# A three-layer kernel: in its last layer the second product takes blocks in another order, Sinkhorn steps are shared between two engines, and weight lows come two slots after highs

## The chip, the cores and the metric

One Trainium2 chip, of which one core runs the whole program. The metric is the time of one execution on the device in microseconds (us). The kernel before takes 1539.9 us, the median of three runs (1539.43 to 1543.54).

## The reference

Three layers follow one another. The first mixes a sequence in the frequency domain (FFT, complex product, shrinking, inverse FFT). The second sends each token to its best of 8 experts, with a capacity. The third, which the change touches, gives every token to every expert, weighted by a Sinkhorn-normalised matrix P:

```python
logits = x @ w_gate
logits = logits - logits.max()
P = np.exp(logits)
for _ in range(8):
    P /= P.sum(1, keepdims=True) + 1e-09
    P /= P.sum(0, keepdims=True) + 1e-09
    P *= N / E
out = np.zeros((N, D), dtype=np.float32)
for e in range(E):
    h = np.maximum(x @ w1[e], 0.0)
    ye = h @ w2[e]
    out += P[:, e:e + 1] * ye
```

Here N is 12288 tokens, of which 3072 slots (8 experts x 384) come out of the second layer with a value other than zero; D is 256, E 8, and 1024 hidden features per expert.

## The kernel before, in words

Products are made at single precision from halves: a value is split into a high part (rounded, in the type fp32r) and a low part (value minus high), and a product is high x high + high x low + low x high, three matmuls.

**Last layer.** The 3072 slots are held transposed, in two sides of 1536 columns. An expert is worked in two halves, and a half in three column tiles of 512, each with two parts `fp` of the features: six units per half, 98 units in all (the last half has its last tile cut into two of 256 columns, so it has eight). In this text units are numbered from 0; units 0 to 11 are the first expert, units 12 to 89 the thirteen halves after it, units 90 to 97 the last half. Within a half, the units of `fp` 0 are the even ones and those of `fp` 1 the odd ones.

The first product of a unit is a 2x2 block product done with seven products (Winograd's form of Strassen's scheme), one in each of seven slots (`PRODS`): three matmuls into a PSUM tile `ps_h` (three buffers). After each slot `post` (L1012) lets ScalarE, VectorE and GpSimd work on it: `plus` (L1032) adds the PSUM tile to a running sum `cc` on VectorE; `high` (L1020) makes the high part of a finished block with ReLU on ScalarE, for two of the four blocks with a second pass (L1022) that leaves ReLU in `cc`; `low` makes the low part, on GpSimd (L1027) or VectorE (L1029). The blocks have the names (f, side): (0,0), (1,1), (0,1), (1,0).

The second product (`second`, L961) of a unit runs in the seven slots of the next unit, three or four of its 24 matmuls behind the first product's three: each of the four blocks is multiplied with two column parts `c` of the weights into four PSUM banks `ps_y`, one per (c, side). The part `fp` 0 begins the banks and `fp` 1 ends them. So a bank begins in an odd unit. `seq` gives the order of the blocks. When a bank is complete, `evict` (L923) takes it out: VectorE multiplies with P (L932) into `yp`, and GpSimd adds that to `acc` (L933); for the first expert the bank is copied or added as it is, and `weigh0` (L937) multiplies it with P later, on GpSimd, in units 12 to 16. The four evictions of a pair of units lie in slots 5 and 6 of an even unit and slots 0 and 1 of the odd unit after it.

**Weights.** Two weight groups are made ready in each half: `load_r` loads one (SP's DMA queue), `sums_r` makes four sums of it on GpSimd (L750 to L753), `split_r` (L756) makes highs on ScalarE (L79) and lows on GpSimd (L80), in three parts.

**Sinkhorn.** After units 0 and 1 the logits' maximum is taken; from unit 2 on one step runs in slot 1 of each unit (`sink_a`, `sink_b`): row sums, a reciprocal, a multiplication of the 128 x 200 matrix `pr`, column sums over it, a matmul with ones that adds over partitions, a reciprocal and a second multiplication, all on VectorE but the matmul. `spread_p` writes P to DRAM, from where it is read back broadcast as `pb`.

**End.** For the last half `finish` (L941) transposes `acc` on TensorE, copies it on ScalarE and scatters rows to the output with indirect DMAs that GpSimd issues (L955), 24 of them.

What each engine does in what order is written out by hand: the code's order is each engine's order. A table of tasks, filled by `at(unit, slot, function)`, places what is not `post` behind a slot; evictions stand ahead of `post` in their slot, tasks behind it.

## Time and profile before

| what | us |
|---|---|
| median of 3 runs | 1539.9 (1539.43 to 1543.54) |
| the profiled execution, its own time | 1528.59 |
| its span, first to last instruction | 1526.7 |
| busy: TensorE matmuls, weight loads | 1433.6, 1198.7 |
| busy: VectorE, ScalarE, GpSimd | 1070.4, 697.4, 915.2 |

The profile is of one execution. Busy time is the sum of an engine's instructions. Its engines are PE (TensorE), PEld (its weight loads, which run beside the matmuls), DVE (VectorE), ACT (ScalarE), POOL (GpSimd) and SP (the queue of DMA issues). PEclk is the granted clock of TensorE as a share of its full speed. L27 would be line 27 of the kernel. A matmul's duration overlaps the next one's; start to start says what it costs.

### The profile page before, as it was taken

The page shows a single profiled execution, that of the slowest core. Times are in us where ns is not written, and L with a number is a line of the kernel's source. Part 1 is how long each engine was busy: PE and PEld are TensorE (multiplying, and loading weights), DVE is VectorE, ACT ScalarE, POOL GpSimd, SP SyncE. Part 2 cuts the span into 40 slices and gives each one's busy share as a digit, 9 for nine tenths or more (in the row PEclk, how much of TensorE's full clock was granted, in tenths as well). Part 3 has the DMA queues.
Part 4 walks back from the last instruction along what each step waited for, and adds up shares of the span by engine and source line. Part 5 has one row for each costly group of instructions (what it writes and reads, how often), then busy time and mean ns, then how long its engine had stood idle before and what let it go on. Part 6 is the DMA issues. An engine that isn't in the chain of part 4 may idle for free.

```text
span 1526.7 us, 20470 instructions
## 1 busy us (share of the span) xinstructions
PE 1433.6 (94%) x7102; PEld 1198.7 (79%) x7102; DVE 1070.4 (70%) x1790; ACT 697.4 (46%) x1326; POOL 915.2 (60%) x921
## 2 busy tenths in 40 slices
PE   8999897999999999999999999999999999999995
PEld 7988785999978777777877777787777778777774
DVE  4768787656579876767667676766767677676773
ACT  3444574555554444444444443444444444444441
POOL 2454356534553458766677677667766766776664
PEclk9999997999999999999999999999999999999997
DMA  9447752633201124322211111011101101110011
GB/s 243 118 127 187 199 173 66 191 104 111 84 28 29 42 72 132 130 72 80 83 44 45 37 42 42 29 42 50 46 31 42 42 31 39 56 42 15 28 53 45
DMA packets 82900, 117.10 MB, mean 77 GB/s; under 512 B 7078, under 2 KB 61190, under 8 KB 81350
## 3 DMA queue, kind: packets, MB, share of 16 engines
q1 hardware_dynamic: 67366, 93.74, 20.1%
q0 software_dynamic: 14656, 21.71, 5.5%
q8 instruction: 57, 0.93, 0.2%
q10 hardware_dynamic: 768, 0.28, 0.2%
q14 instruction: 53, 0.43, 0.1%
HBM read 87.29 MB, written 28.41 MB: 76 GB/s over the span
## 4 chain that ended last, share of the span: by engine, by line
PE 60%; POOL 12%; ACT 4%; DVE 4%; issue 3%; DMA 0%; POOLq 0%; DVEq 0%; ACTq 0%
PE ps_y L979 27%; PE ps_h L1089 24%; PE ps_h L686 4%; PE ps_yT L735 3%; POOL h L1027 3%; POOL acc L933 3%; POOL w L1027 2%; POOL w L80 2%; DVE cc L1032 2%; ACT cc L1022 1%; POOL zl L80 1%; ACT h L1020 1%; PE lg L700 1%; ACT w L79 1%; ACT w L1020 1%
## 5 line engine op out<-in xcount | busy, mean ns | idle before, releaser
L1032 DVE TENSOR_TENSOR cc<-ps_h,cc 128x512 f32<-128x512 f32 (+1 forms) x686 | 455.0, 677 | 288.4 <-PE ps_h L1089 273.7
L1020 ACT ACTIVATE h<-cc 128x512 fp32r<-128x512 f32 (+1 forms) x197 | 122.9, 624 | 338.0 <-DVE cc L1032 335.7
L933 POOL TENSOR_TENSOR acc<-acc,yp 128x512 f32<-128x512 f32 x162 | 236.5, 1473 | 21.7 <-DVE yp L932 21.7
L979 PE MATMUL ps_y<-h,w 128*128 128x512 f32 (+1 forms) x732 | 221.1, 392 | 8.2 <-POOL h L1027 8.2
L1089 PE MATMUL ps_h<-b_hi,w 128*128 128x512 f32 (+1 forms) x544 | 212.2, 391 | 0.0
L979 PEld LDWEIGHTS ps_y<-h,w 128*128 128x128 f32 x732 | 136.9, 193 | 42.1 <-POOL h L1027 13.7
L1089 PE MATMUL ps_h<-t_x,w 128*128 128x512 f32 (+1 forms) x544 | 168.2, 391 | 1.5 <-DVE cc L1032 1.5
L1020 ACT ACTIVATE w<-cc 128x512 fp32r<-128x512 f32 (+1 forms) x130 | 81.1, 624 | 192.0 <-DVE cc L1032 191.0
L1022 ACT ACTIVATE cc<-cc 128x512 f32<-128x512 f32 (+1 forms) x196 | 122.4, 625 | 6.2
L1089 PEld LDWEIGHTS ps_h<-t_x,w 128*128 128x128 f32 x544 | 102.2, 190 | 24.1 <-DVE cc L1032 1.9
L1089 PEld LDWEIGHTS ps_h<-b_hi,w 128*128 128x128 f32 x544 | 103.8, 191 | 21.9 <-DVE cc L1032 0.3
L932 DVE TENSOR_TENSOR yp<-ps_y,pb 128x512 f32<-128x512 f32 (+1 forms) x172 | 114.7, 667 | 7.0 <-PE ps_y L979 6.4
L979 PE MATMUL ps_y<-zl,w 128*128 128x512 f32 (+1 forms) x360 | 114.1, 389 | 5.0 <-POOL zl L1027 5.0
L979 PE MATMUL ps_y<-w 128*128 128x512 f32 (+1 forms) x274 | 104.4, 395 | 15.2 <-POOL w L1027 15.2
L979 PE MATMUL ps_y<-w,w 128*128 128x512 f32 (+1 forms) x266 | 101.7, 396 | 12.3 <-POOL w L1027 12.3
L80 POOL TENSOR_TENSOR w<-rw,w 128x128 fp32r<-128x128 f32 (+2 forms) x60 | 49.6, 840 | 95.7 <-ACT w L79 95.7
L1089 PE MATMUL ps_h<-b_lo,w 128*128 128x512 f32 (+1 forms) x272 | 106.2, 390 | 0.0
L979 PE MATMUL ps_y<-h,zl 128*128 128x512 f32 x320 | 97.8, 394 | 3.0 <-POOL h L1027 3.0
L1089 PE MATMUL ps_h<-b_hi,zl 128*128 128x512 f32 x240 | 95.1, 396 | 0.0
L979 PE MATMUL ps_y<-w,zl 128*128 128x512 f32 x240 | 80.8, 402 | 12.6 <-POOL w L1027 12.6
L1027 POOL TENSOR_TENSOR h<-cc,h 128x512 fp32r<-128x512 f32 (+1 forms) x66 | 86.7, 1323 | 5.5 <-ACT cc L1022 5.3
L979 PEld LDWEIGHTS ps_y<-zl,w 128*128 128x128 f32 x360 | 67.0, 191 | 22.2 <-POOL zl L1027 9.4
(265 smaller groups left out, 3271.3 us busy)
## 6 DMA issues: line engine op xcount, KB each, us to landing
pb<-p_d SPq DMA_DIRECT2D x44, 512.0 KB, 3.8
rw<-in_moe_w_dram SPq DMA_DIRECT2D x60, 256.0 KB, 3.1
raw<-in_moe_w_dram SPq DMA_DIRECT2D x26, 512.0 KB, 4.7
out_dram<-zt SPq DMA_DIRECT2D x24, 512.0 KB, 5.3
mf<-in_c_mats_dram POOLq DMA_DIRECT2D x40, 192.0 KB, 3.1
ds<-d SPq DMA_DIRECT2D x48, 128.0 KB, 2.8
xc<-ds SPq DMA_DIRECT2D x8, 768.0 KB, 6.2
xs_d<-xo SPq DMA_DIRECT2D x32, 192.0 KB, 3.1
```

The costliest lines, as they stand in the source:

```text
L79: nc.scalar.copy(hi_ap, src)
L80: (lo_engine or nc.vector).tensor_sub(lo_ap, src, hi_ap.bitcast(F32))
L686: nc.tensor.matmul(ps[:, 0:cap], l, r[:, h, :], start=k == 0, stop=k == 5)
L735: nc.tensor.matmul(yT[e][c], l, r, start=fk == 0 and i == 0, stop=fk == 2 * NF - 1 and i == 2)
L932: nc.vector.tensor_mul(y[:, 0:n], ps[:, 0:n], pbs[e, c0][:, side, 0:n])
L933: (nc.vector if last else nc.gpsimd).tensor_add(a, a, y[:, 0:n])
L979: yield lambda l=l, r=r, c=c, side=side, st=st, sp_=fp == 1 and k == final[side] and i == 2: nc.tensor.matmul(banks[c, side][:, 0:n], l, r ...
L1020: nc.scalar.activation(hs[f, side][0][:, 0:n], cc[k][:, 0:n], AF.Relu)
L1022: nc.scalar.activation(cc[k][:, 0:n], cc[k][:, 0:n], AF.Relu)
L1027: eng.tensor_sub(hl[:, 0:n], cc[k][:, 0:n], hh[:, 0:n].bitcast(F32))
L1032: nc.vector.tensor_add(cc[d][:, 0:n], ps[:, 0:n], cc[a][:, 0:n])
L1089: nc.tensor.matmul(ps[:, 0:n], l, x_[:, c0:c0 + n], start=k == 0, stop=k == 2)
```

## The change

- The second product takes the blocks as (0,0), (1,1), (1,0), (0,1), for both parts `fp`. Products six and seven of the first product change places, and with them the slots in which (1,0) and (0,1) are finished. Evictions take side 0 ahead of side 1.
- GpSimd's low of block (1,1) moves from slot 5 to slot 4. VectorE's lows are now (1,0) in slot 6 and (0,1) in slot 0 of the next unit.
- In the last half all lows and all additions to `acc` are VectorE's, and ScalarE's second pass is left out there.
- A Sinkhorn step stands in three places of a unit (slots 1, 3 and 6), and GpSimd does its two multiplications.
- Evictions of the first expert's second half are a copy on ScalarE and an addition on GpSimd, in place of an addition on VectorE.
- `split_r` issues the highs of a part in one slot and its lows two slots later; the sums move from slot 0 to slot 3.
- The transposes of `finish` use the PSUM tile of the small products for all but one in two, and stand in every second slot.

Instructions by engine, counted in the two programs. VectorE has 16 multiplications of `pr` and 12 additions from PSUM fewer; it has 8 block lows of 512 and 8 of 256 columns more, and 6 additions to `acc` more (4 of 512 columns, 2 of 256). GpSimd gives up those lows and those 6 additions and gets the 16 multiplications and 12 additions to `acc`. ScalarE has 12 copies of a bank more and 16 second passes fewer. TensorE's matmuls are the same in number, and the DMA issues of SP and GpSimd the same in number and order.

The diff, cut to its core:

```diff
-    def split_r(r, t, u, part):
+    def split_r(r, t, u, part, which=None):
...
-            split(w[:, o:o + n], w[:, WN + o:WN + o + n], src, nc.gpsimd)
+            if which != 1:
+                nc.scalar.copy(w[:, o:o + n], src)
+            if which != 0:
+                nc.gpsimd.tensor_sub(w[:, WN + o:WN + o + n], src, w[:, o:o + n].bitcast(F32))
...
-    def sink_a():
+    def sink_a1():
...
-        nc.vector.tensor_tensor(pr, pr, rs.unsqueeze(2).to_broadcast([128, NT + 1, E]), op=ALU.mult)
+        nc.gpsimd.tensor_tensor(pr, pr, rs.unsqueeze(2).to_broadcast([128, NT + 1, E]), op=ALU.mult)
+
+    def sink_a2():
         cs = hp.tile([128, E], F32, tag="cs", name="cs", bufs=2)
...
-    def sink_b(cs):
+    def sink_b():
...
-        nc.vector.tensor_tensor(pr, pr, rc.unsqueeze(1).to_broadcast([128, NT + 1, E]), op=ALU.mult)
+        nc.gpsimd.tensor_tensor(pr, pr, rc.unsqueeze(1).to_broadcast([128, NT + 1, E]), op=ALU.mult)
...
+        y = hp.tile([128, BL], F32, tag="py", name="yp", bufs=3)
         if e == 0:
-            nc.vector.tensor_add(a, ps[:, 0:n], a)
+            nc.scalar.copy(y[:, 0:n], ps[:, 0:n])
+            nc.gpsimd.tensor_add(a, a, y[:, 0:n])
             return
...
-        seq = [((1, 1), (0, 1), (0, 0), (1, 0)), ((0, 0), (1, 1), (0, 1), (1, 0))][fp]
+        seq = ((0, 0), (1, 1), (1, 0), (0, 1))
...
-    PRODS = ((0, B11), (4, T2), (1, B21), (5, T3), (3, T1), (6, B22), (2, T4))
+    PRODS = ((0, B11), (4, T2), (1, B21), (5, T3), (3, T1), (2, T4), (6, B22))
...
-                at(first + 1, 0, lambda r=r: sums_r(r))
-                for k, i in enumerate((0, 4, NS + 2)):
-                    at(first + 2, i, lambda r=r, k=k: split_r(r, rws[r], sus[r], k))
+                at(first + 1, 3, lambda r=r: sums_r(r))
+                for k, i in enumerate((1, 3, NS + 1)):
+                    for which in range(2):
+                        at(first + 2, i + 2 * which, lambda r=r, k=k, which=which: split_r(r, rws[r], sus[r], k, which))
...
-    for k, fn in enumerate(sink):
-        at(2 + k, 1, fn)
-    n_s = 2 + len(sink)
+    at(2, 1, sink_exp)
+    for k in range(ITERS):
+        at(2 + k, 3, sink_a1)
+        at(2 + k, 6, sink_a2)
+        at(3 + k, 1, sink_b)
+    at(2 + ITERS, 4, spread_p)
+    n_s = 4 + ITERS
...
+        end = units[u][0:2] == (E - 1, 1)
+        mid = nc.vector if end else nc.gpsimd
...
-            low(0, 0, 0, nc.gpsimd)
+            low(0, 0, 0, mid)
         elif i == 4:
             plus(3, 2)
-            high(3, 1, 1)
+            high(3, 1, 1, not end)
             plus(1, 1)
+            low(3, 1, 1, mid)
         elif i == 5:
+            plus(2, 2)
+            high(2, 1, 0)
+        else:
             plus(1, 1)
             high(1, 0, 1)
-            low(3, 1, 1, nc.gpsimd)
-        else:
-            plus(2, 2)
-            high(2, 1, 0)
-            low(1, 0, 1, nc.vector)
-            at(u + 1, 0, lambda: low(2, 1, 0, nc.vector))
+            low(2, 1, 0)
+            at(u + 1, 0, lambda: low(1, 0, 1))
...
-                when = {(0, 1): (u, 5), (1, 1): (u, 6), (0, 0): (u + 1, 0), (1, 0): (u + 1, 1)}
+                when = {(0, 0): (u, 5), (1, 0): (u, 6), (0, 1): (u + 1, 0), (1, 1): (u + 1, 1)}
```

How the order of instructions moves, at three places. In the names, `cc` are running sums, `h0` to `h4` and the upper ends of `w1`, `w2` and `zl` the six buffer pairs of highs and lows, `rw` and `su` weights as loaded and their sums, `ps_y_...` PSUM banks.

GpSimd in unit 44, the third of a half, and the first part of unit 45, before. The block lows are lines L1027, those of (0,0) and (1,1) in turn:

```order
L80 TENSOR_TENSOR w2_7237<-rw_12787,w2_7237 128x128
L80 TENSOR_TENSOR w2_7237<-rw_12787,w2_7237 128x256
L1027 TENSOR_TENSOR w1_7236<-cc_12961,h4_8958 128x512
L80 TENSOR_TENSOR w2_7237<-su_12876,w2_7237 128x512
L933 TENSOR_TENSOR acc_8953<-acc_8953,yp_13021 128x512
L1027 TENSOR_TENSOR w2_7237<-cc_13006,w1_7236 128x512
L933 TENSOR_TENSOR acc_8953<-acc_8953,yp_13034 128x512
L933 TENSOR_TENSOR acc_8953<-acc_8953,yp_13048 128x512
L933 TENSOR_TENSOR acc_8953<-acc_8953,yp_13066 128x512
L80 TENSOR_TENSOR w2_7237<-rw_12787,w2_7237 128x512
```

And in the changed kernel, where block lows are L1031, weight lows L764, additions L931:

```order
L1031 TENSOR_TENSOR w1_7236<-cc_12985,h4_8958 128x512
L764 TENSOR_TENSOR w2_7237<-rw_12811,w2_7237 128x128
L764 TENSOR_TENSOR w2_7237<-rw_12811,w2_7237 128x256
L1031 TENSOR_TENSOR w2_7237<-cc_13031,w1_7236 128x512
L931 TENSOR_TENSOR acc_8953<-acc_8953,yp_13045 128x512
L764 TENSOR_TENSOR w2_7237<-su_12940,w2_7237 128x512
L931 TENSOR_TENSOR acc_8953<-acc_8953,yp_13058 128x512
L931 TENSOR_TENSOR acc_8953<-acc_8953,yp_13072 128x512
L931 TENSOR_TENSOR acc_8953<-acc_8953,yp_13091 128x512
L1031 TENSOR_TENSOR h1_8955<-cc_13075,h0_8954 128x512
L764 TENSOR_TENSOR w2_7237<-rw_12811,w2_7237 128x512
```

The low of (1,1), `w2_7237<-cc_...`, stood behind the weight low of `su` and an addition; now it stands ahead of both, and behind the two small weight lows.

TensorE at the start of unit 45, before, the first matmuls of the second product (of unit 44); `w2_7237` as the moving operand's name is the low of (1,1):

```order
L979 MATMUL ps_y_13044<-w1_7236,zl_2920 128x512
L979 MATMUL ps_y_13044<-w2_7237,zl_2920 128x512
L979 MATMUL ps_y_13044<-w1_7236,zl_2920 128x512
L1089 MATMUL ps_h_13057<-t_x_7330,w1_7236 128x512 x3
L979 MATMUL ps_y_13061<-w1_7236,zl_2920 128x512
L979 MATMUL ps_y_13061<-w2_7237,zl_2920 128x512
L979 MATMUL ps_y_13061<-w1_7236,zl_2920 128x512
L979 MATMUL ps_y_13044<-w2_7237,zl_2920 128x512
L1089 MATMUL ps_h_13071<-b_hi_7328,w1_7236 128x512
L1089 MATMUL ps_h_13071<-b_lo_7329,w1_7236 128x512
L1089 MATMUL ps_h_13071<-b_hi_7328,w1_7236 128x512
L979 MATMUL ps_y_13044<-zl_2920 128x512
```

And in the changed kernel, where `h4` and `w1` are high and low of (0,0), and `w1` and `w2` those of (1,1):

```order
L978 MATMUL ps_y_13068<-h4_8958,zl_2920 128x512
L978 MATMUL ps_y_13068<-w1_7236,zl_2920 128x512
L978 MATMUL ps_y_13068<-h4_8958,zl_2920 128x512
L1095 MATMUL ps_h_13081<-t_x_7330,w1_7236 128x512 x3
L978 MATMUL ps_y_13085<-h4_8958,zl_2920 128x512
L978 MATMUL ps_y_13085<-w1_7236,zl_2920 128x512
L978 MATMUL ps_y_13085<-h4_8958,zl_2920 128x512
L978 MATMUL ps_y_13089<-w1_7236,zl_2920 128x512
L1095 MATMUL ps_h_13097<-b_hi_7328,w1_7236 128x512
L1095 MATMUL ps_h_13097<-b_lo_7329,w1_7236 128x512
L1095 MATMUL ps_h_13097<-b_hi_7328,w1_7236 128x512
L978 MATMUL ps_y_13089<-w2_7237,zl_2920 128x512
```

The block (0,0) is now first, the low of (1,1) is read for the first time behind 16 other matmuls of the unit, and the seventh matmul of the second product begins a bank of the other side; the bank after it begins at the tenth.

VectorE at the end of unit 92 and the start of unit 93, in the last half, before (multiplications L932, lows L1029, additions to `acc` L933):

```order
L932 TENSOR_TENSOR yp_17247<-ps_y_17104,pb_17138 128x512
L1032 TENSOR_TENSOR cc_17204<-ps_h_17239,cc_17204 128x512
L932 TENSOR_TENSOR yp_17260<-ps_y_17118,pb_17138 128x512
L1032 TENSOR_TENSOR cc_17224<-ps_h_17253,cc_17224 128x512
L1029 SCALAR_TENSOR_TENSOR zl_2920<-cc_17204,w2_7237 128x512
L932 TENSOR_TENSOR yp_17274<-ps_y_17146,pb_17138 128x512
L933 TENSOR_TENSOR acc_8953<-acc_8953,yp_17274 128x512
L1029 SCALAR_TENSOR_TENSOR zl_2920<-cc_17224,zl_2920 128x512
L932 TENSOR_TENSOR yp_17289<-ps_y_17157,pb_17138 128x512
L933 TENSOR_TENSOR acc_8953<-acc_8953,yp_17289 128x512
```

And in the changed kernel (L927, L1033, L929):

```order
L927 TENSOR_TENSOR yp_17266<-ps_y_17126,pb_17161 128x512
L929 TENSOR_TENSOR acc_8953<-acc_8953,yp_17266 128x512
L1036 TENSOR_TENSOR cc_17243<-ps_h_17258,cc_17243 128x512
L927 TENSOR_TENSOR yp_17278<-ps_y_17140,pb_17161 128x512
L929 TENSOR_TENSOR acc_8953<-acc_8953,yp_17278 128x512
L1036 TENSOR_TENSOR cc_17224<-ps_h_17271,cc_17224 128x512
L1033 SCALAR_TENSOR_TENSOR zl_2920<-cc_17243,w2_7237 128x512
L927 TENSOR_TENSOR yp_17292<-ps_y_17144,pb_17161 128x512
L929 TENSOR_TENSOR acc_8953<-acc_8953,yp_17292 128x512
L1033 SCALAR_TENSOR_TENSOR zl_2920<-cc_17224,zl_2920 128x512
L927 TENSOR_TENSOR yp_17308<-ps_y_17157,pb_17161 128x512
L929 TENSOR_TENSOR acc_8953<-acc_8953,yp_17308 128x512
```

Each of the four multiplications of an eviction now has its addition behind it on VectorE; one low stands ahead of the third multiplication and one between the third and the fourth, as before.

## Rows read from the trace of the kernel before

**Rows 1.** windows by stage of the last layer: span, then busy us (instructions), PEclk, DMA, GB/s
```profile
422.65:555.36 132.71, 125.78 (x557) 100.16 (x556) 109.01 (x205) 64.90 (x119) 61.68 (x61) 1.00 0.12 38
555.36:1422.16 866.80, 826.51 (x3512) 662.43 (x3511) 616.42 (x859) 376.03 (x650) 597.51 (x529) 0.99 0.17 54
1443.39:1526.70 83.31, 61.24 (x343) 54.04 (x341) 44.77 (x83) 26.43 (x55) 42.85 (x42) 0.85 0.13 45
```

**Rows 2.** windows of units 42 to 47, then of unit 51
```profile
889.30:899.59 10.29, 10.29 (x47) 8.45 (x46) 8.11 (x12) 4.86 (x8) 5.95 (x6) 1.00 0.11 32
899.59:910.51 10.92, 10.67 (x47) 8.37 (x46) 8.57 (x12) 4.28 (x7) 10.20 (x11) 1.00 0.21 68
910.51:920.80 10.29, 10.29 (x46) 8.44 (x45) 7.06 (x12) 5.35 (x10) 3.35 (x4) 1.00 0.00 0
920.80:935.75 14.95, 12.24 (x47) 9.51 (x46) 7.79 (x12) 4.87 (x8) 11.37 (x10) 0.89 0.18 64
935.75:946.15 10.40, 10.40 (x46) 8.44 (x45) 7.25 (x12) 4.34 (x7) 5.35 (x7) 1.00 0.03 11
946.15:956.80 10.65, 10.65 (x47) 8.36 (x45) 8.34 (x12) 5.25 (x10) 8.96 (x8) 1.00 0.14 49
...
988.30:1001.58 13.28, 10.57 (x47) 8.37 (x45) 7.76 (x12) 4.87 (x8) 11.30 (x10) 1.00 0.20 70
```

**Rows 3.** waits of TensorE in units 12 to 89: total us, times, longest
```profile
PE ps_y L979 <- POOL w L1027: 35.3, 13, 2.7
PE ps_y L979 <- POOL h L1027: 5.0, 13, 1.9
```

**Rows 4.** timeline of GpSimd at unit 45: start us, us, line, operation
```profile
919.90 1.30 POOL L80 TENSOR_TENSOR w<-su,w 128x512 fp32r<-128x512 f32 x1 [2.18 <-ACT w L79]
921.17 1.72 POOL L933 TENSOR_TENSOR acc<-acc,yp 128x512 f32<-128x512 f32 x1
922.85 1.71 POOL L1027 TENSOR_TENSOR w<-cc,w 128x512 fp32r<-128x512 f32 x1
```

**Rows 5.** timeline of TensorE at unit 45
```profile
924.61 0.73 PE L979 MATMUL ps_y<-w,zl 128*128 128x512 f32 x2 [2.71 <-POOL w L1027]
```

**Rows 6.** timeline of ScalarE in unit 43
```profile
905.80 0.63 ACT L1022 ACTIVATE cc<-cc 128x512 f32<-128x512 f32 x1
```

**Rows 7.** timeline of VectorE at the start of unit 43
```profile
899.76 1.65 DVE L1029 SCALAR_TENSOR_TENSOR w<-cc,h 128x512 fp32r<-128x512 f32 x1
901.33 0.68 DVE L932 TENSOR_TENSOR yp<-ps_y,pb 128x512 f32<-128x512 f32 x1
901.93 1.18 DVE L1029 SCALAR_TENSOR_TENSOR w<-cc,w 128x512 fp32r<-128x512 f32 x1
903.03 0.68 DVE L932 TENSOR_TENSOR yp<-ps_y,pb 128x512 f32<-128x512 f32 x1
```

**Rows 8.** timeline of VectorE, its longest and its shortest low
```profile
603.56 1.78 DVE L1029 SCALAR_TENSOR_TENSOR w<-cc,w 128x512 fp32r<-128x512 f32 x1
...
910.62 0.68 DVE L1029 SCALAR_TENSOR_TENSOR h<-cc,h 128x512 fp32r<-128x512 f32 x1
```

**Rows 9.** waits of TensorE in units 0 to 11
```profile
PE ps_y L979 <- POOL w L1027: 3.1, 2, 1.7
PE ps_y L979 <- POOL h L1027: 2.0, 1, 2.0
```

**Rows 10.** groups by line, units 0 to 11: busy us, mean ns, idle before
```profile
L845 DVE TENSOR_TENSOR pr<-pr,rs 128x200 f32<-128x200 f32 x8 | 2.9, 367 | 0.3
...
L80 POOL TENSOR_TENSOR w<-rw,w 128x256 fp32r<-128x256 f32 x2 | 1.5, 744 | 0.0
```

**Rows 11.** group of VectorE from 1443.39 on, and timeline of the last matmuls
```profile
L1032 DVE TENSOR_TENSOR cc<-ps_h,cc 128x256 f32<-128x256 f32 x28 | 11.4, 422 | 14.5 <-PE ps_h L1089 14.3
...
1510.76 2.45 PE L979 MATMUL ps_y<-h,w 128*128 128x256 f32 x12
```

More of the change, by code (lines that the diff above doesn't have):

```diff
@@ L848, in sink_a @@
         nc.vector.scalar_tensor_tensor(cs, pr[:, NT, :], WZ, cs, op0=ALU.mult, op1=ALU.add)
-        return cs
-    def sink_b(cs):
+        state["cs"] = cs
+    def sink_b():
         ps = pq.tile([128, NT, 2 * E], F32, tag="s", name="ps_s")
-        nc.tensor.matmul(ps[:, 0, 0:E], ones_f, cs, start=True, stop=True)
+        nc.tensor.matmul(ps[:, 0, 0:E], ones_f, state["cs"], start=True, stop=True)
         rc = hp.tile([128, E], F32, tag="rc", name="rc", bufs=2)
@@ L857, in sink_b @@
         nc.vector.tensor_scalar_mul(rc, rc, float(N // E))
-        nc.vector.tensor_tensor(pr, pr, rc.unsqueeze(1).to_broadcast([128, NT + 1, E]), op=ALU.mult)
+        nc.gpsimd.tensor_tensor(pr, pr, rc.unsqueeze(1).to_broadcast([128, NT + 1, E]), op=ALU.mult)
     state = {}
-    def sink_rows():
-        state["cs"] = sink_a()
-    def sink_cols(last):
-        sink_b(state["cs"])
-        if not last:
-            sink_rows()
-    sink = [lambda: (sink_exp(), sink_rows())] + [lambda k=k: sink_cols(k == ITERS - 1) for k in range(ITERS)]
     p_d = dr.tile([E, S], F32, name="p_d")
@@ L927, in evict @@
             return
+        y = hp.tile([128, BL], F32, tag="py", name="yp", bufs=3)
         if e == 0:
[L929 removed]
+            nc.scalar.copy(y[:, 0:n], ps[:, 0:n])
+            nc.gpsimd.tensor_add(a, a, y[:, 0:n])
             return
[L931 removed]
         nc.vector.tensor_mul(y[:, 0:n], ps[:, 0:n], pbs[e, c0][:, side, 0:n])
[L933 removed]
+        if last:
+            nc.vector.tensor_add(a, a, y[:, 0:n])
+        else:
+            nc.gpsimd.tensor_add(a, a, y[:, 0:n])
     def weigh0(c, side, c0):
@@ L941, in finish @@
     def finish(c0, side, g):
-        pt = ph.tile([128, 2, D], F32, tag="h", name="ps_o")
+        pt = (pq.tile([128, 2, D], F32, tag="s", name="ps_o") if len(outs) != 1 else
+              ph.tile([128, 2, D], F32, tag="h", name="ps_o"))
         if not outs:
@@ L1014, in tile_c, with high @@
             return hp.tile([128, BL], F32, tag="cc", name="cc", bufs=5)
-        def high(k, f, side):
+        def high(k, f, side, also=False):
             nonlocal npair
@@ L1020, in high, with low @@
             nc.scalar.activation(hs[f, side][0][:, 0:n], cc[k][:, 0:n], AF.Relu)
-            if k in (0, 3):
+            if also:
                 nc.scalar.activation(cc[k][:, 0:n], cc[k][:, 0:n], AF.Relu)
-        def low(k, f, side, eng):
+        def low(k, f, side, eng=nc.vector):
             hh, hl = hs[f, side]
@@ L1069, in tile_spectral_mix__moe_topk__moe_sinkhorn @@
             last = (pe_, ph_) == (E - 1, 1)
-            fins = [(side, g) for side in (1, 0) for g in range(pn // 256)]
+            fins = [(side, g) for side in (0, 1) for g in range(pn // 256)]
             if u == NU2:
-                when = {(c, side): (u, NS) for c in range(2) for side in range(2)}
+                when = {(c, side): (u, NS) for side in range(2) for c in range(2)}
             else:
-                when = {(0, 1): (u, 5), (1, 1): (u, 6), (0, 0): (u + 1, 0), (1, 0): (u + 1, 1)}
+                when = {(0, 0): (u, 5), (1, 0): (u, 6), (0, 1): (u + 1, 0), (1, 1): (u + 1, 1)}
             for (c, side), (uu, i) in when.items():
                 soon.setdefault((uu, i), []).append(
-                    lambda c=c, side=side, a=(pe_, ph_, pc, pn), last=last and (side == 0 or u == NU2): evict(*a, c, side, banks[c, side], last))
+                    lambda c=c, side=side, a=(pe_, ph_, pc, pn), last=last: evict(*a, c, side, banks[c, side], last))
             if last:
                 for k, (side, g) in enumerate(fins):
-                    at(u + 1, (3 if u < NU2 else 0) + k, lambda pc=pc, side=side, g=g: finish(pc, side, g))
+                    at(u + 1, 3 + 2 * k if u < NU2 else k, lambda pc=pc, side=side, g=g: finish(pc, side, g))
         if u < NU2 and fp == 0 and e > 0:
```

8 lines of the change are left out of this document (3 added, 5 removed).

## The prediction

> **What bounds the kernel now.** I read the windows by stage first. The last layer runs from 422.65 to 1526.70 us of the span, 72% of it, and in its long middle, units 12 to 89, TensorE is busy for 826.5 of 866.8 us [rows 1]. TensorE sets the end there; the question is what its lost time is. The six units of one half of an expert answer it: they do equal work (45 matmuls of 512 columns) and take 10.29, 10.92, 10.29, 14.95, 10.40 and 10.65 us; the fourth of the next half takes 13.28 [rows 2]. I take 10.28 us as the undisturbed unit (0.2285 us a matmul). The long ones are the second, fourth and sixth (the odd units), and the longest has a granted clock of 0.89, where the next half's fourth has 1.00. The 78 units of the middle then hold 78 x 10.28 = 801.8 us of matmuls, and 65.0 us are lost, 5.0 per half.
>
> The waits of TensorE name who ends it: 40 us on GpSimd's lows [rows 3], in each half 2.7 us in the fourth unit and about 0.4 in the second. The timeline shows why. GpSimd runs a weight low (L80), an accumulation (L933) and only then the block low (L1027), which ends at 924.56 [rows 4]; TensorE does one matmul of the second product, waits 2.71 us and starts again at 924.61 [rows 5], for a stretch at the lower of its two levels, 1.2 GHz, by the granted clock of that unit [rows 2]. The low is that of block (1,1), made late and by the even units consumed first. The second unit's wait leaves the clock at 1.00, and so does the long wait of the next half: 14.95 against 13.28 us says that a fall costs 1.6 us where it comes.
>
> **The change, part by part.** *Order of the blocks and of GpSimd's queue.* In the third unit of a half the low of (1,1) moves from behind a weight low of 1.30 and an addition of 1.72 us to ahead of both, and its first reader moves from number 1 to number 7 (counted from 0) of the next unit's second product, with 16 matmuls or 3.7 us of that unit ahead of it; the block read at once is now (0,0), whose low stands first. The low of (0,0) can start when ScalarE's second pass ends, 906.43 in the unit that began at 899.59, so 6.8 us into a unit [rows 6]; at 1.3 us it ends at 8.1 and is needed at 10.5. Two small weight lows, at most 1.5 us together by the larger one's 0.74 [rows 10], follow, then low (1,1), until 10.9 at the latest, needed at 13.9. Both are early by 2 us or more. Four 128x128 sums in their place, at most 3.0 us by the same row, leave 1.5. So the waits of rows 3 should go. The queue still holds the same work: 46 of 66.7 us a half [rows 1]; what is late next is an addition, for which only PSUM banks wait.
>
> *Those banks are the new wait.* Each odd unit starts the next use of four banks. The pair evicted last was needed at matmuls 12 and 15 of the second product; now it is needed at matmuls 6 and 9, that is 12 and 18 matmuls into the unit: 2.74 and 4.11 us. VectorE's queue there is low, multiplication, low, multiplication, unchanged. In the unit that starts at 899.59 the two multiplications end at 902.01 and 903.71, or +2.42 and +4.12 us [rows 7]. So the second one is just in time. A low takes 0.68 us alone and up to 1.78 [rows 8]; the unit of rows 7 had 1.65 + 1.18. From below the cost is nothing; from above, with 1.78 twice, the end moves by 0.73 to +4.85, a wait of 0.74 in 39 odd units, 29 us. I take 0.5 us per half, 6.5 us, near the lower end, the side that the rows of such a place lie on [rows 7].
>
> The rule that speaks against the change is in the Trainium skill, "SBUF — State Buffer", section "Who interferes with whom": a VectorE instruction with two SBUF inputs and a GpSimd instruction that reads SBUF exclude each other, and the later one blocks until the other ends. The trace agrees in kind (0.68 against 1.78 us). By the row the term is 6.5 us; by the rule, with a whole GpSimd instruction ahead of every low, it would be the 44 us of rival 2.
>
> Units 12 to 17 also carry the 12 weighing multiplications on GpSimd; I leave them 2 us of waits. Middle: 65.0 - 6.5 - 2 = **56.5 us** gained.
>
> *Weight lows two slots after the highs, sums later.* No operation is added. GpSimd no longer stands waiting for a copy that ScalarE has not begun; that idle time ended nothing by itself, so I count it at nothing beyond the above. The target buffer is free throughout: its last reader is done a unit earlier. SP's and GpSimd's DMA issues keep their order and number, so no transfer moves past another.
>
> *Sinkhorn and first expert (units 0 to 11).* They take 132.7 us against 123.4, 9.3 more; TensorE's waits for GpSimd's lows are 5.1 of them [rows 9], the rest is extra TensorE work there (logits, sums over partitions) and a first wait. VectorE loses two multiplications of 0.37 us per step [rows 10] and twelve additions from PSUM. GpSimd gets them, ScalarE a copy ahead of each addition; ScalarE is busy for 64.9 of these 132.7 us [rows 1] and takes it beside other work. What a 128x200 multiplication costs on GpSimd no row shows: between VectorE's 0.37 and the 0.74 of a 128x256 subtraction on GpSimd [rows 10], I take 0.7, nearest to the row of its own engine. New waits: TensorE's product for the column sums now comes two slots after those sums, which VectorE makes behind a low. With rows 7 the low ends at +1.74, the reduction and its correction (two instructions of 0.37 or little more) at +2.6 at the latest, and TensorE arrives at +2.97. That is no wait; if GpSimd delivers its multiplication 1 us late in each of eight steps it is 8 us. Between -2 and +7 I take **5 us** gained, nearer the upper end, because the multiplication has three slots, some 4.4 us, for its 0.7.
>
> *Last half and tail.* From 1443.39 to the end there are 83.3 us [rows 1] at a granted clock of 0.85. The change puts all lows and all additions on VectorE. From there its queue holds 38 instructions of 512 columns at 0.69 and 52 of 256 at 0.42 [rows 7, 11]: 26.2 + 21.8 = 48.0 us. TensorE's own matmuls up to the last product, at 0.2285 us and half of it for 256 columns, are 20.6 + 7.9 + 15.4 = 43.9 us, so VectorE becomes the bound there. With 2.3 us until its first instruction (nine matmuls), 4 for waits on ScalarE's highs, 2 for the last product and the 13.5 us from its last matmul (1513.2 [rows 11]) to the end, I get 69.8, 13.5 less. I take **12 us**, since waits around 2 us appear where both engines are full and may cost a stretch at 1.2 GHz. Bounds: 2 if the clock falls as often as now, 17 if nothing waits.
>
> **Sum.** 56.5 + 5 + 12 = 73.5 us. The profiled execution took 1528.6 us (span 1526.7), so it should become 1455. The median of the runs shown is 1539.9, 0.7% above it; I keep the difference: 1466.
>
> **Rivals.**
> 1. *Banks wait at the rows' maximum.* 29 us in the middle instead of 6.5, Sinkhorn 3, tail 9: 34 + 12 = 46 gained, 1494. For it: the second multiplication has no slack in rows 7. Against: a low alone takes 0.68 [rows 8].
> 2. *Every VectorE low waits for a whole GpSimd instruction*, 0.68 + 1.29 = 1.97. To the 2.83 us of the two lows of rows 7 that adds 1.11 us per odd unit, 43 to 44 in all: 19 + 12 = 31 gained, 1509. For it: lows of 1.65 and 1.78 exist [rows 7, 8]. Against it: none reaches 1.97. [...]
> 3. *The bank wait grows over 2.1 us and lowers the clock.* With both lows behind a GpSimd instruction that was itself held (1.72), they take 2.4 each and the second multiplication ends at +6.1. 39 x 2.0 is 78 us against 65 + 17 gained at best; from 2.1 us per odd unit on it is a loss. If every second wait costs 1.6 us of clock as now, 31 more: 27 slower, 1567. For it: three such waits a half instead of one. Against: the longest low of the rows is 1.78 [rows 8].
> 4. *The change doesn't do what it says:* the lows are held by ScalarE's second pass rather than by GpSimd's queue, and TensorE waits as before; 1536 to 1541. Against: GpSimd worked from 919.90 to 924.56 without a gap [rows 4].
>
> **How the numbers follow.** Forecast 0.70, rival 1 0.15, rival 2 0.07, rival 3 0.04, rival 4 0.03, more than the best bounds 0.01. The forecast's best case is 65 + 8 + 17 = 90 us, 1450; its poor case 54, 1486. The range takes in rival 1 and the worst of the bounds: 1449 to 1500. About 0.3% (4.6 us) can be told from no change: faster 0.93, same 0.03, slower 0.04.
>
> **What would show it.** Right: the odd units at 10.3 to 10.6 us, no wait of TensorE on GpSimd's lows in the middle, granted clock 1.00 there, units 12 to 89 near 810 us. Rival 1 or 2: waits of the second product's matmuls on VectorE's multiplication, 0.5 to 1.1 us in odd units, lows over 1.7. Wrong on Sinkhorn: TensorE waiting for the column sums. Wrong on the tail: more than 72 us from unit 92 on. A middle above 840 us refutes the forecast.

## Result and profile after

The changed kernel takes 1472.9 us, the median of four executions (1469.51 to 1474.01), beside 1540.1 for the kernel before: a ratio of 0.9556, interval 0.9534 to 0.9577. The forecast was 1466 with a range from 1449 to 1500. The profiled execution took 1472.11 us.

The windows of the changed kernel by stage of the last layer (units 0 to 11, 12 to 89, 90 and 91, 92 to the end); the columns are those of [rows 1]:

```profile
435.99:562.95 126.96, 124.49 (x556) 100.55 (x556) 101.22 (x181) 68.64 (x127) 78.75 (x86) 1.00 0.16 51
562.95:1375.99 813.04, 810.97 (x3511) 656.66 (x3510) 622.89 (x855) 380.53 (x654) 586.68 (x532) 1.00 0.17 56
1375.99:1397.18 21.19, 20.93 (x91) 16.82 (x90) 18.28 (x27) 6.63 (x11) 8.37 (x7) 1.00 0.07 26
1397.18:1469.90 72.72, 57.46 (x343) 49.52 (x341) 48.65 (x101) 20.77 (x43) 24.54 (x24) 0.93 0.15 51
```

Against [rows 1] the middle gives 53.8 us, the first expert 5.75, the end 10.6; the whole last layer goes from 1104.05 to 1033.91 us, 70.1 less. TensorE is now busy for 811.0 of the middle's 813.0 us. One number does not belong to the change: the last layer starts at 435.99, where it started at 422.65. The code ahead of it is the same; the last section comes back to it.

The windows of units 42 to 47, which answer to [rows 2], and of unit 14:

```profile
878.26:888.54 10.28, 10.28 (x47) 8.45 (x45) 7.89 (x12) 4.89 (x8) 5.21 (x6) 1.00 0.04 12
888.54:899.02 10.48, 10.48 (x46) 8.37 (x45) 8.44 (x12) 4.29 (x7) 9.40 (x10) 1.00 0.28 90
899.02:909.32 10.30, 10.30 (x46) 8.44 (x45) 7.50 (x12) 5.36 (x10) 4.59 (x6) 1.00 0.00 1
909.32:919.62 10.30, 10.30 (x47) 8.37 (x45) 8.36 (x12) 4.88 (x8) 10.30 (x8) 1.00 0.16 52
919.62:930.02 10.40, 10.40 (x46) 8.44 (x45) 7.26 (x12) 4.34 (x7) 4.86 (x8) 1.00 0.15 50
930.02:940.46 10.44, 10.44 (x47) 8.37 (x45) 8.41 (x12) 5.36 (x10) 9.44 (x8) 1.00 0.15 50
583.64:597.76 14.12, 12.19 (x46) 9.51 (x45) 7.50 (x12) 5.41 (x10) 13.08 (x15) 0.88 0.53 151
```

The fourth unit, 14.95 us before, takes 10.30, at a granted clock of 1.00. The reason is in GpSimd's timeline around the end of unit 44, which answers to [rows 4]:

```profile
907.92 1.30 POOL L1031 TENSOR_TENSOR w<-cc,w 128x512 fp32r<-128x512 f32 x1 [0.55 <-ACT cc L1026]
909.17 1.30 POOL L931 TENSOR_TENSOR acc<-acc,yp 128x512 f32<-128x512 f32 x1
910.43 1.75 POOL L764 TENSOR_TENSOR w<-su,w 128x512 fp32r<-128x512 f32 x1
```

The low of (1,1) ends at 909.22, 10.20 us into its unit (899.02), where it ended 14.05 us into it before; it waits for ScalarE alone, and the addition and the weight low stand behind it. Three lines of the waits in the middle are what is left for the second product (one more, of 0.6 us, stands at a weight load); [rows 3] had 40.3 us on GpSimd's lows at the matmuls:

```profile
PEld ps_y L978 <- DVE yp L927: 9.2, 38, 0.3
PEld ps_y L978 <- POOL zl L1031: 2.3, 1, 2.3
PE ps_y L978 <- POOL zl L1031: 1.9, 1, 1.9
```

The first line is the forecast's new wait, for the banks, in 38 odd units, 0.24 us each; it is so short that it shows at the weight loads and not at the matmuls. The other two are one wait on a low of GpSimd, in unit 14, the last of the windows above; the part on why the prediction was right comes back to it. VectorE's timeline at the start of unit 43 (888.54), which answers to [rows 7]:

```profile
888.71 1.62 DVE L1033 SCALAR_TENSOR_TENSOR w<-cc,h 128x512 fp32r<-128x512 f32 x1
890.25 0.68 DVE L927 TENSOR_TENSOR yp<-ps_y,pb 128x512 f32<-128x512 f32 x1
890.85 1.18 DVE L1033 SCALAR_TENSOR_TENSOR w<-cc,w 128x512 fp32r<-128x512 f32 x1
891.95 0.68 DVE L927 TENSOR_TENSOR yp<-ps_y,pb 128x512 f32<-128x512 f32 x1
```

The two multiplications end 2.39 and 4.09 us into the unit and are needed at 2.74 and 4.11, to a few hundredths what [rows 7] had.

Of the signs that the prediction named, the odd units (10.29 to 10.49 us) and the middle (813) came as it said. Two did not: TensorE does wait once for a low of GpSimd, in unit 14, where the clock falls to 0.88, and the end, at 72.7 us, lies just beyond the 72 that it called wrong.

### The profile page after: what moved, and what is told of

Read it like the earlier page. It is cut to its first block, busy times and chain, and to the rows that moved or that the text cites. A ratio compares the mean times of both kernels' runs of the same rounds, so it can differ in the third digit from the quotient of the medians.

```text
span 1469.9 us, 20547 instructions
## 1 busy us (share of the span) xinstructions
PE 1415.6 (96%) x7102; PEld 1188.3 (81%) x7102; DVE 1074.7 (73%) x1784; ACT 697.1 (47%) x1322; POOL 896.0 (61%) x927
## 4 chain that ended last, share of the span: by engine, by line
PE 70%; issue 5%; POOL 5%; DVE 1%; ACT 1%; DMA 0%; POOLq 0%; DVEq 0%; ACTq 0%
PE ps_y L978 32%; PE ps_h L1095 28%; PE ps_h L686 5%; PE ps_yT L735 4%; POOL out_dram L954 1%; PE lg L700 1%; POOL acc L925 1%; POOL acc L931 1%; POOL acc L935 0%; PE ps_t L674 0%; POOL w L764 0%; DVE cc L1036 0%; DMA xg<-xs_d,idx 0%; POOL h L1031 0%; POOL xg L719 0%
## 5 line engine op out<-in xcount | busy, mean ns | idle before, releaser
L931 POOL TENSOR_TENSOR acc<-acc,yp 128x512 f32<-128x512 f32 x156 | 226.7, 1481 | 7.2 <-DVE yp L927 7.2
L978 PE MATMUL ps_y<-h,w 128*128 128x512 f32 (+1 forms) x732 | 216.2, 387 | 0.3 <-DVE yp L927 0.3
L1031 POOL TENSOR_TENSOR h<-cc,h 128x512 fp32r<-128x512 f32 x60 | 78.1, 1302 | 70.4 <-ACT cc L1026 70.3
L1026 ACT ACTIVATE cc<-cc 128x512 f32<-128x512 f32 x180 | 114.2, 635 | 5.7
L927 DVE TENSOR_TENSOR yp<-ps_y,pb 128x512 f32<-128x512 f32 (+1 forms) x172 | 115.0, 668 | 1.3 <-PE ps_y L978 1.3
L1031 POOL TENSOR_TENSOR zl<-cc,w 128x512 fp32r<-128x512 f32 x30 | 38.8, 1293 | 85.9 <-ACT cc L1026 85.9
L1031 POOL TENSOR_TENSOR w<-cc,h 128x512 fp32r<-128x512 f32 x30 | 38.9, 1298 | 85.0 <-ACT cc L1026 85.0
```

The lines of the kernel that those rows point to most:

```text
L927: nc.vector.tensor_mul(y[:, 0:n], ps[:, 0:n], pbs[e, c0][:, side, 0:n])
L931: nc.gpsimd.tensor_add(a, a, y[:, 0:n])
L978: yield lambda l=l, r=r, c=c, side=side, st=st, sp_=fp == 1 and k == final[side] and i == 2: nc.tensor.matmul(banks[c, side][:, 0:n], l, r ...
L1026: nc.scalar.activation(cc[k][:, 0:n], cc[k][:, 0:n], AF.Relu)
L1031: eng.tensor_sub(hl[:, 0:n], cc[k][:, 0:n], hh[:, 0:n].bitcast(F32))
```

## Experiments

Since the first part of the program varied, stages of the last layer are compared, each from one profile. In e5 to e8, v7 and v8 the kernel before took 1529 to 1530 us beside them, in the others 1540 to 1541. In the profiles of these others the end holds a wait that the profile doesn't explain: unit 96 takes 9.4 to 10.6 us in them and 6.2 to 6.3 in e8, v7 and v8 (last section). So ends are best compared within a group; the profile of the kernel before belongs with e5 to e8, v7 and v8. What each label stands for is told below the table.

| kernel | units 0-11 | 12-89 | 92-end | last layer | ratio to before, interval |
|---|---|---|---|---|---|
| before | 132.7 | 866.8 | 83.3 | 1104.1 | 1 |
| changed | 127.0 | 813.0 | 72.7 | 1033.9 | 0.9556 (0.9534 to 0.9577) |
| e1 | 127.0 | 809.9 | 75.4 | 1033.0 | 0.9512 (0.9472 to 0.9552) |
| e2 | 127.7 | 812.5 | 71.9 | 1033.7 | 0.9546 (0.9524 to 0.9568) |
| e3 | 127.0 | 814.6 | 72.5 | 1036.0 | 0.9547 (0.9521 to 0.9573) |
| e4 | 128.8 | 867.1 | 73.5 | 1091.1 | 0.9912 (0.9883 to 0.9941) |
| e5 | 128.6 | 813.2 | 79.4 | 1042.0 | 0.9581 (0.9548 to 0.9613) |
| e6 | 129.9 | 807.6 | 77.6 | 1035.9 | 0.9552 (0.9518 to 0.9586) |
| e7 | 133.2 | 820.7 | 80.8 | 1055.8 | 0.9673 (0.9642 to 0.9704) |
| e8 | 128.5 | 812.9 | 70.0 | 1032.6 | 0.9530 (0.9496 to 0.9563) |
| v1 | 126.9 | 812.2 | 70.8 | 1031.1 | 0.9524 (0.9494 to 0.9554) |
| v2 | 127.2 | 808.5 | 73.8 | 1030.6 | 0.9510 (0.9482 to 0.9537) |
| v7 | 127.7 | 809.5 | 66.7 | 1025.0 | 0.9485 (0.9466 to 0.9504) |
| v8 | 127.7 | 809.5 | 66.6 | 1025.0 | 0.9488 (0.9463 to 0.9513) |

**e1 to e3: one part put back.** Theory A is that each of three parts (reading order, low ahead, spacing of the weight lows) by itself takes the low of (1,1) off the path; theories B, C and D are that one of them did it.

e1, on the changed kernel (with the slots of products six and seven and the evictions' sides):

```diff
-        seq = ((0, 0), (1, 1), (1, 0), (0, 1))
+        seq = [((1, 1), (0, 1), (0, 0), (1, 0)), ((0, 0), (1, 1), (0, 1), (1, 0))][fp]
...
```

> The changed kernel with only the order of the blocks put back (reading order, the two products, the evictions' sides); the low of (1,1) stays ahead in slot 4. Units 12 to 89 take 813.0 us in the changed kernel. Theory A (each of the parts by itself takes the low of (1,1) off the path): in the changed kernel this low ends 10.2, 10.8 and 11.3 us after the start of its unit, and with the old reading order it is needed at 11.2, so 0.1 us per half is waited for, and the banks are needed later: 811 to 816 us. Theory B (it is the reading order that removed the waits): the 40 us of waits on GpSimd's lows come back, with falls of the clock: 840 us or more.

e2:

```diff
         elif i == 4:
...
-            low(3, 1, 1, mid)
         elif i == 5:
             plus(2, 2)
             high(2, 1, 0)
+            low(3, 1, 1, mid)
```

> The changed kernel with only GpSimd's low of (1,1) put back to slot 5, behind an addition. Theory A (each part by itself suffices): it ends at most 1.7 us later, 12 to 13 us after its unit's start, and is needed at 13.9: units 12 to 89 stay at 812 to 815 us. Theory C (it is the place in GpSimd's queue that removed the waits): 840 us or more.

e3:

```diff
-                at(first + 1, 3, lambda r=r: sums_r(r))
-                for k, i in enumerate((1, 3, NS + 1)):
...
+                at(first + 1, 0, lambda r=r: sums_r(r))
+                for k, i in enumerate((0, 4, NS + 2)):
+                    at(first + 2, i, lambda r=r, k=k: split_r(r, rws[r], sus[r], k))
```

> The changed kernel with only the weight groups put back: highs and lows of a part issued together in the old slots, sums in slot 0. Theory A (each part by itself suffices; the spacing of the weight lows ended nothing): GpSimd waits again for ScalarE's high ahead of a weight low, up to 2.2 us, but behind the low of (1,1); units 12 to 89 at 812 to 816 us. Theory D (the spacing removed the waits): 830 us or more, with TensorE waiting on GpSimd's lows.

The middle took 809.9, 812.5 and 814.6 us, the last two where theory A had them and e1 1 us below; B, C and D fall. In e1 the bank waits are gone as well, so it is 3.2 us shorter than the changed kernel. In e3 GpSimd stands again behind ScalarE's weight highs, and from unit 18 on no matmul waits for it (ahead of that two do, 1.7 and 1.1 us):

```profile
POOL w L764 <- ACT w L762: 59.4, 24, 5.4
POOL zl L764 <- ACT zl L762: 35.0, 13, 5.3
```

These are two lines of GpSimd's waits in e3's middle; the changed kernel has none of them.

**e5 to e7: one part alone, on the kernel before.**

```diff
e5 (with the products, the evictions' sides and VectorE's lows)
-        seq = [((1, 1), (0, 1), (0, 0), (1, 0)), ((0, 0), (1, 1), (0, 1), (1, 0))][fp]
+        seq = ((0, 0), (1, 1), (1, 0), (0, 1))
...
e6 (whole)
             plus(1, 1)
+            low(3, 1, 1, nc.gpsimd)
         elif i == 5:
             plus(1, 1)
             high(1, 0, 1)
-            low(3, 1, 1, nc.gpsimd)
...
e7 (with split_r's new argument, the new slots and the sums in slot 3)
-                    at(first + 2, i, lambda r=r, k=k: split_r(r, rws[r], sus[r], k))
+                        at(first + 2, i + 2 * which, lambda r=r, k=k, which=which: split_r(r, rws[r], sus[r], k, which))
...
```

> The kernel before with only the new order of the blocks (reading order, products six and seven, evictions' sides); low of (1,1) in slot 5, weight groups, Sinkhorn and last half's engines as before. Units 12 to 89 took 866.8 us before, 813.0 in the changed kernel. Theory A (each part by itself suffices): the low of (1,1) ends 14.05 us after the start of its unit in the trace before, behind the weight low and the addition, and is now needed at 13.94; the wait is 0.1 us in one unit of a half: 811 to 818 us. Rival (a part does little without the others): 835 us or more.

> The kernel before with only GpSimd's low of (1,1) moved from slot 5 to slot 4, ahead of the weight low and the addition. Theory A: it then ends 10 to 11.3 us after its unit's start and is needed at 11.2 by the old order: 810 to 818 us in units 12 to 89. Rival (a part does little without the others): 835 us or more.

> The kernel before with only the weight groups changed: highs two slots ahead of lows, sums in slot 3. The low of (1,1) stays in slot 5 but the large weight low comes behind it; one addition stays ahead. It should end 11.6 to 12 us after its unit's start and is needed at 11.2: the fourth unit of a half then waits about 0.4 us as the second and sixth do, with the clock at 1.00. Theory A: 815 to 830 us in units 12 to 89. The prediction's count of this part at nothing would give 860 or more when it stands alone.

The windows of their units 12 to 89, one kernel after the other:

```profile
549.16:1362.37 813.21, 811.65 (x3512) 656.20 (x3510) 619.05 (x859) 376.27 (x650) 598.12 (x529) 1.00 0.17 57
```

```profile
548.48:1356.10 807.62, 806.20 (x3511) 658.41 (x3510) 624.98 (x859) 376.19 (x650) 593.00 (x529) 1.00 0.18 58
```

```profile
554.04:1374.74 820.70, 816.71 (x3511) 655.56 (x3510) 617.79 (x859) 377.92 (x650) 582.06 (x529) 1.00 0.17 57
```

So the parts give 53.6, 59.2 and 46.1 us alone and 53.8 together: they are three ways of removing one wait, and their gains don't add. The largest is a low written one slot earlier; e6 as a whole has the ratio of the full change. (e6 came out 2 us below its expected window: with the old order no bank is waited for, and unit 14 takes 10.30 us there, as in e5 and e7, against 14.12 in the changed kernel.) In e7 GpSimd's timeline, again at the end of unit 44 (which starts at 891.28 there), has the order that its expectation gave:

```profile
900.04 1.30 POOL L936 TENSOR_TENSOR acc<-acc,yp 128x512 f32<-128x512 f32 x1 [0.41 <-DVE yp L935]
901.30 1.29 POOL L1031 TENSOR_TENSOR w<-cc,w 128x512 fp32r<-128x512 f32 x1
902.55 1.74 POOL L764 TENSOR_TENSOR w<-su,w 128x512 fp32r<-128x512 f32 x1
```

The low ends 11.3 us into the unit (11.6 to 12 was expected), needed at 11.2: a fourth unit of 10.51 us.

**e4: the bank wait made large.** On the changed kernel:

```diff
-            at(u + 1, 0, lambda: low(1, 0, 1))
+            low(1, 0, 1)
```

> The changed kernel with VectorE's low of (0,1) moved ahead of the two multiplications that free the PSUM banks, so that the first of them ends some 3.6 us into an odd unit, where the bank is needed at 2.74. The prediction's bank wait, made large: by its arithmetic 0.8 us of wait in each of 39 odd units of the middle, 31 us, so units 12 to 89 at 840 to 848 us, at a granted clock of 1.00. Rival 3's mechanism (such waits lower the clock): a fall of 1.6 us in every second unit that waits, 870 us or more. If the banks are not what TensorE needs there: no change, 813.

The middle took 867.1 us, all that the change had gained there. VectorE at the start of unit 43 (903.61), TensorE's wait in the middle, and the window of the middle:

```profile
903.78 1.61 DVE L1033 SCALAR_TENSOR_TENSOR w<-cc,h 128x512 fp32r<-128x512 f32 x1
905.31 1.78 DVE L1033 SCALAR_TENSOR_TENSOR w<-cc,w 128x512 fp32r<-128x512 f32 x1
907.01 1.27 DVE L927 TENSOR_TENSOR yp<-ps_y,pb 128x512 f32<-128x512 f32 x2
```

```profile
PE ps_y L978 <- DVE yp L927: 48.3, 38, 1.3
```

```profile
558.45:1425.51 867.06, 816.82 (x3511) 656.75 (x3510) 639.75 (x855) 379.73 (x654) 577.24 (x533) 1.00 0.16 52
```

The mechanism is the prediction's, and its price was too low: I took 1.18 us for the second low, it took 1.78, the first multiplication ends 4.07 us into the unit instead of 3.6, and TensorE waits 1.27 us 38 times where 0.8 was expected. The granted clock stays at 1.00 in every unit that waits so; it falls in unit 14 alone, as in the changed kernel. Waits of this length cost themselves and little more (54 us in all, for 48.3 of wait), so the clock part of rival 3 doesn't come at 1.3 us.

**v2: the bank wait taken away.**

```diff
-            at(u + 1, 0, lambda: low(1, 0, 1))
+            at(u + 1, 1, lambda: low(1, 0, 1))
```

> The changed kernel with VectorE's low of (0,1) moved from ahead of the last multiplication of an eviction to behind it (slot 1 of the next unit). Units 12 to 89 take 813.0 us in the changed kernel; 807.6 and 809.9 in the two kernels that kept the old reading order with the low of (1,1) ahead. Theory E (what is left in the odd units, 10.48, 10.30 and 10.45 us against 10.28, is the bank wait): the second multiplication ends some 1.1 us earlier, and the three come to 10.3 to 10.4: 808 to 811. Rival (it is something else, such as the weight loads): 812 to 814.

The middle took 808.5 us and the line of 9.2 us at the weight loads is gone. The second, fourth and sixth units went, in the mean of 13 halves, from 10.48, 10.30 and 10.45 to 10.41, 10.28 and 10.30: 3.1 us in all. That is the bank wait as it was. The rest of the 4.6 us is a fall of the clock in unit 14 that this execution didn't have (below). The end took 73.8 us, within what six kernels with the same engines there show (70.0 to 75.4).

**e8: Sinkhorn's multiplications on VectorE.**

```diff
-        nc.gpsimd.tensor_tensor(pr, pr, rs.unsqueeze(2).to_broadcast([128, NT + 1, E]), op=ALU.mult)
+        nc.vector.tensor_tensor(pr, pr, rs.unsqueeze(2).to_broadcast([128, NT + 1, E]), op=ALU.mult)
```

> The changed kernel with Sinkhorn's two multiplications back on VectorE, still in three places of a unit. Units 0 to 11 took 132.7 us before and 127.0 in the changed kernel. Theory A (the gain there came from GpSimd's lows, whose waits were 5.1 us): 126.5 to 128 us. Rival (it came from giving the multiplications to GpSimd): 130 us or more. Units 12 to 89 at 813 in both.

128.5 us, just beyond theory A's window: of the 5.75 us that the changed kernel gains there the place of the multiplications carries 1.5. e5 and e6, with Sinkhorn and first expert as before, gain 4.1 and 2.8 us there, so about half or more of the gain comes with the lows; e7 gains nothing there (133.2). Some 0.8 us lie in units 0 and 1 (19.45 us in the kernel before and e5 to e7, 18.61 to 18.91 in all others), which goes with a line of the diff that the first part doesn't list: it spreads what the layer ahead left to do over the slots of unit 0. No run has it by itself.

```diff
-        at(0, k, fn)
+        at(0, 1 + 3 * k, fn)
```

**v1, v7, v8: the end, and a better version.** v1 leaves the last half's additions on GpSimd but for the last four:

```diff
+            end_ = u == NU2
...
-                    lambda c=c, side=side, a=(pe_, ph_, pc, pn), last=last: evict(*a, c, side, banks[c, side], last))
+                    lambda c=c, side=side, a=(pe_, ph_, pc, pn), last=end_: evict(*a, c, side, banks[c, side], last))
```

> The changed kernel with the last half's additions to the accumulator on GpSimd again, but for the four behind the last product; its lows stay on VectorE. From unit 92 to the end the changed kernel took 72.7, 71.9, 72.5, 73.5 and 70.0 us in five profiles. Theory A (VectorE's queue sets the bank waits there, 1.5 us in unit 93 and 2.3 us in unit 95): without 0.6 and 0.35 us of addition ahead of each later multiplication they shrink by some 2 us: 68 to 71. Rival (GpSimd's additions stretch VectorE's lows as in the middle and take it back): 71.5 to 74.

70.8 us, in theory A's window, though within the 70.0 to 73.5 us that the same code shows without it; the total settles nothing. The units that the expectation named do: unit 93 takes 11.62 to 11.64 us in v1, v7 and v8 and 12.31 to 13.16 in the six kernels with the changed kernel's order and end (the changed kernel, e2, e3, e4, e8, v2), unit 95 takes 7.97 to 7.98 against 8.42 to 10.14. v7 puts together v1, v2's low (not in the last half) and a later `spread_p`:

```diff
-    at(2 + ITERS, 4, spread_p)
+    at(3 + ITERS, 1, spread_p)
...
-            at(u + 1, 0, lambda: low(1, 0, 1))
+            at(u + 1, 0 if end else 1, lambda: low(1, 0, 1))
```

> A version made from the findings: the changed kernel with the low of (0,1) behind the last multiplication of an eviction (not in the last half), the last half's additions on GpSimd but for the last four, and the spreading of P one unit later (unit 11, slot 1), where the transposes' wait of 1.1 us on VectorE in unit 10 should go. Theory A: units 0 to 11 at 125 to 126 us (127.0 in the changed kernel), 12 to 89 at 808 to 809 (813.0), from 92 on at 70 to 71.5 (72.7); the last layer 1026 to 1029 us against 1033.9. Rival (P then comes late, and GpSimd's weighing with it): units 12 to 17 lose what unit 10 gains, 12 to 89 at 810 to 813.

v8 adds buffers for the output rows:

```diff
+            if fin[0] in (0, 5):
+                outs.append(hp.tile([128, 512], F32, tag="su", name="o2"))
...
```

> The same with five or six in place of four buffers for the output rows of the last half. Theory F (ScalarE's copy waits for the scatter of an earlier row block to free its buffer, and TensorE behind it, 0.6 to 2.1 us in the tails seen): from unit 92 on 1 to 2 us less than in the version before it. Rival (the wait moves to the next scatter, since GpSimd issues them one by one): no difference beyond 1 us.

The last window of v7, from unit 92 on, and of e8, which has the changed kernel's end; the kernel before took about the same time beside both (1530 and 1529):

```profile
1378.03:1444.70 66.67, 54.99 (x343) 48.01 (x341) 44.55 (x89) 20.91 (x43) 38.51 (x36) 0.95 0.17 56
```

```profile
1386.26:1456.30 70.04, 56.98 (x343) 49.42 (x341) 48.79 (x101) 20.77 (x43) 24.28 (x24) 0.93 0.15 53
```

3.4 us less, with 4.2 us less of VectorE's work: units 93 and 95 are 1.2 and 2.2 us shorter, the second with a fall of the clock to 0.83 in e8 that v7 doesn't have. There VectorE's queue does bound the time, and GpSimd can carry the additions. v7's last layer is 1025.0 us, 8.9 below the changed kernel and 7.6 below e8. Its ratio of 0.9485 lies 0.7% below the changed kernel's, with intervals that don't overlap, though those executions are of the other group; beside e8 it is 0.45%, and the intervals overlap. With v8 it has the shortest last layer of all. The later `spread_p` missed: unit 10 went from 12.6 to 11.0 us, but unit 11 from 10.3 to 12.4. v8 equals v7 (66.6 and 66.7), and theory F falls where it could be looked at: in v7 no copy waited for a buffer.

## Why the prediction was right

*What bounds the kernel.* Right: TensorE's own matmuls, with GpSimd's lows ending its waits. Taken away, TensorE is busy for 99.7% of the middle.

*Order of the blocks and of GpSimd's queue.* "So the waits of rows 3 should go": they went, 40.3 to 1.9 us. The forecast had the low of (1,1) end 10.9 us into the unit at the latest, needed at 13.9; it ended at 10.2 in the unit reckoned. (The low of (0,0) is needed at 11.2 by the same count, not at 10.5; that only adds room.) What it didn't say is that either half of that sentence would have done (e1, e2, e5, e6).

*The banks.* "I take 0.5 us per half, 6.5 us": 3.1 us (v2). The step was right in kind and place and twice too large. Rivals 1 and 2 needed lows of 1.78 in both places or longer. Rival 2's 0.68 + 1.29 = 1.97 is reached by none of the 156 lows in the changed kernel's middle, whose longest is 1.78. The rows say why: the 120 lows that begin while a GpSimd instruction runs all end 0.55 us after it (0.545 to 0.553), and the 36 others take 0.68 us. VectorE's two lows at the start of unit 18, and what GpSimd ran beside the first (beside the second it ran nothing):

```profile
629.45 1.77 DVE L1033 SCALAR_TENSOR_TENSOR zl<-cc,w 128x512 fp32r<-128x512 f32 x1
631.14 0.68 DVE L1033 SCALAR_TENSOR_TENSOR zl<-cc,zl 128x512 fp32r<-128x512 f32 x1
```

```profile
629.37 1.30 POOL L764 TENSOR_TENSOR w<-su,w 128x512 fp32r<-128x512 f32 x1
```

So a low waits for what is left of the GpSimd instruction that it meets, from all of it to nothing, and rival 2 priced all of it for every low. The Trainium skill's rule ("SBUF — State Buffer", "Who interferes with whom"), by which the later of the two blocks until the other ends, agrees with these rows; what failed is the price that rival 2 took from it.

*Units 12 to 17.* "I leave them 2 us": 4.3, of which 3.8 in unit 14, where TensorE waits 1.93 us for the low of (1,1) and the clock falls, and 0.4 in unit 16. Lines of GpSimd's timeline there (the unit starts at 583.64):

```profile
579.07 2.56 POOL L925 TENSOR_TENSOR acc<-acc,yp 128x512 f32<-128x512 f32 x2
581.57 1.31 POOL L935 TENSOR_TENSOR acc<-acc,pb 128x512 f32<-128x512 f32 x1
582.83 1.30 POOL L1031 TENSOR_TENSOR zl<-cc,w 128x512 fp32r<-128x512 f32 x1
...
586.79 1.28 POOL L935 TENSOR_TENSOR acc<-acc,pb 128x512 f32<-128x512 f32 x1
588.03 1.27 POOL L1031 TENSOR_TENSOR zl<-cc,zl 128x512 fp32r<-128x512 f32 x1
```

The first expert's additions (L925), which the change gave to GpSimd, run on into unit 13 among the weighing (L935) and push its two lows back, the second behind the four weight sums as well (the lines left out). In e5, e6 and e7, where VectorE still does these additions, unit 14 takes 10.30 us, in e7 with the sums in the same slot. The forecast priced the weighing and forgot that these additions stand with it. The second and the fifth unit of a half keep 0.12 us each, 3.1 in all, even in v2; that was in no term. 3.1 + 4.3 + 3.1 = 10.5 of the 11.2 us left, against 8.5. That the two sums lie so close is in part luck: the bank wait was taken 3.4 us too large, and the 3.1 us that no term held nearly fill that.

*Weight lows two slots after the highs.* The forecast said "that idle time ended nothing by itself, so I count it at nothing beyond the above". The sum is about right (e3: 1.6 us, or 3.2 without the fall of the clock in unit 14, which e3 didn't have), the reason is not: alone the spacing takes 46.1 of the 54 us (e7), because the large weight low, which stood ahead of the block low while it waited for ScalarE, now stands behind it. GpSimd's waits of this kind in the middle before, 166 us:

```profile
POOL w L80 <- ACT w L79: 108.2, 44, 4.4
POOL zl L80 <- ACT zl L79: 57.8, 22, 4.4
```

*Sinkhorn and first expert.* 5 us against 5.75. "I take 0.7" for a multiplication of `pr` on GpSimd was above what it takes, 0.54 and 0.62 us:

```profile
L863 POOL TENSOR_TENSOR pr<-pr,rc 128x200 f32<-128x200 f32 x8 | 5.0, 619 | 20.7 <-PE ps_h L1095 14.1 <-DVE rc L862 6.6
...
L848 POOL TENSOR_TENSOR pr<-pr,rs 128x200 f32<-128x200 f32 x8 | 4.3, 537 | 0.0
```

*Last half.* 12 us against 10.6, and VectorE is busy for 48.65 us where the forecast counted 48.0. The profile of the changed kernel holds waits in unit 96 that e8, with the same end, doesn't have:

```profile
ACT h L1024 <- issue: 4.2, 1, 4.2
DVE cc L1036 <- remote: 2.4, 1, 2.4
PE ps_h L1095 <- issue: 1.7, 1, 1.7
```

Here "issue" and "remote" are waits for which the profile names no instruction. The unit takes 10.22 us there and 6.26 in e8, whose end takes 70.0 us from unit 92 on, 13.3 less than before and below the 72 of the prediction's sign. What the change took away is TensorE's waits on GpSimd's lows, none of which is left; before, from unit 92 on, they were 10.7 us:

```profile
PE ps_y L979 <- POOL zl L1027: 5.0, 2, 3.2
PE ps_y L979 <- POOL h L1027: 4.0, 2, 3.4
PE ps_y L979 <- POOL w L1027: 1.7, 1, 1.7
```

Waits of 3.0 us on VectorE's multiplications came instead. e5, e6 and e7, with the end's engines as before, keep 6.5, 5.3 and 10.7 us of the waits on lows and take 79.4, 77.6 and 80.8 us. No run separates the move of the lows from the new place of the transposes, so how the gain divides between them is not shown.

*Sum.* 70.1 us in the last layer against 73.5. Of the 6.9 us by which the time lies above the forecast, 3.4 are these terms. The other 3.5 I put, by subtraction, ahead of the last layer: I carried over the 0.7% (11 us) between the profile and the median of the kernel before as if it were fixed, but the part ahead took 418.6 to 436.0 us in the profiles here, 13.3 more in that of the changed kernel than in that of the kernel before. (In the best case of the forecast, 65 + 8 + 17, the 8 should be the 7 of its own bounds; nothing hangs on it.)
